# A cross network on one core: the first rows loaded by columns, and the corner matmuls behind the row tiles

## The chip, the core and the metric

The kernel runs on one core of a Trainium2 chip. The metric is the device time of one execution in microseconds. The core has a matrix engine (TensorE, PE in the profile; its weight loads are PEld), three engines for elementwise work (VectorE or DVE, ScalarE or ACT, GpSimd or POOL), a synchronisation engine (SyncE or SP) and 16 DMA engines. Loads are issued here from SP and from ScalarE, each into a queue of its own.

## The reference

Six cross layers of a recommender network, on 4096 rows of 416 features, all in bfloat16:

```python
B, F, D, L = 4096, 26, 16, 6
Din = min(F * D, 1024)          # 416
# x0: (B, Din), ws: (L, Din, Din), bs: (L, Din)
x = x0
for l in range(ws.shape[0]):
    x = x0 * (x @ ws[l] + bs[l]) + x
return x
```

The kernel uses that, up to rounding, x after layer l is x0 times a factor that grows by x @ ws + bs in each layer. It keeps x @ ws accumulated over the layers in PSUM, with the biases summed up over the layers.

## The kernel before

**Layout.** Activations lie transposed: features on the 128 partitions, rows along the free dimension. The 416 features are three chunks of 128 (0, 1, 2) and a rest of 32, called the tail. The 4096 rows are four groups (p) of 1024, each of two blocks of 512. The tail of a group's four quarters of 256 rows lies packed on 4×32 partitions. A layer's weights therefore fall into four kinds of matmul:

- *mains*: chunk by chunk, 128×128 pieces of the weights, written as 32-column tiles four at a time (`main`, with `columns` at L330 and `again` at L310, which uses the weights already held). Layer 0 of the first group, first block, is done instead in `first` with whole 128×128 matmuls (L288).
- *row tiles*: from the tail to the three chunks, 32-row tiles (L391).
- *column tiles*: from the three chunks to the tail, 32-column tiles (L406).
- the *corner*: from the tail to the tail, as a block-diagonal 128×128 matrix `wc_sb` in 32-column tiles (L387, recorded at the helper's L330). ScalarE builds it out of `w3_sb`, four copies a layer (`corner`, L531).

**Order.** For each group p and layer l, with n = 6p + l: mains of block 0, then `tail` (corner, row tiles, column tiles), then mains of block 1. The order is written out by hand and kept by semaphores. TensorE counts up `s_pe` four times a layer: behind the row tiles, behind the column tiles, and behind the second and third chunk of block 1. VectorE waits for these and forms the next x in six steps a layer (L490, L499). ScalarE (L545) and GpSimd (L234) share a seventh piece, the third chunk of block 0.

**The start.** The first 512 rows come in row-major form (`xin_sb`) in two loads of 256 rows, one from SP (L135), one from ScalarE (L516). TensorE issues 22 warm-up matmuls on ones (`idle`, L244), then transposes the rows chunk by chunk (`turn`, L256, four transposes each), and VectorE copies each transposed chunk from PSUM to `x0T_sb` (L473). `biases` (L265, L271) sums up the biases of the layers with seven small matmuls; VectorE copies these to `cb_sb` (L478). `first` then runs layer 0's mains chunk by chunk (k = 0, 1, 2), each behind its weights (`s_w0[k]`) and its copied chunk (`s_ev`). Turn 2 and two transposes of the tails (L299) stand behind the mains of k = 0. The rest of the first 1024 rows is transposed by a DMA (L144), and SP's queue then has the weights of the layers 1 to 5 (L148 for the chunks, L151 for the tail weights). Layer 0's tail weights come in four loads of 26 KB (`tails0`, L77), two from SP and two from ScalarE.

## Time and profile before

| what | value |
|---|---|
| runs | 131.56, 132.18, 132.2 us; median 132.18 |
| the profiled execution | 131.24 us, its span 129.5 us |
| mean granted clock of TensorE | 0.994 |
| TensorE busy | 124.4 us (96%) |
| VectorE busy | 93.7 us (72%) |
| ScalarE, GpSimd busy | 25.5 us (20%), 30.2 us (23%) |
| TensorE on the chain of waits | 93% |

The span goes from the first to the last instruction; the execution's time has some 1.7 us around it. The three runs are without a profile. Times in the text are microseconds from the start of the span. Matmuls overlap in the array, so the length of one (0.27 us for 256 columns) is longer than the distance between the starts of two (0.11 us at full clock). Line numbers are those of the kernel before.

### The profile page before, as it was taken

What the parts mean: (1) busy time and instruction counts of PE and PEld (TensorE: products, weight loads), DVE (VectorE), ACT (ScalarE), POOL (GpSimd) and SP (SyncE); (2) the same over time, 40 slices, a digit from 0 to 9 for tenths busy, and PEclk for the clock granted to TensorE, in tenths of its full rate; (3) what the DMA queues carried; (4) which work ended last, traced back from release to release, by engine and by line L of the source; (5) the groups of instructions that cost most, each with busy time, mean ns of one, the idle gap of its engine ahead of it and who ended that gap; (6) DMA issues with size and microseconds to landing.
All of it is one profiled execution on the core that took longest, in us unless ns stands there. A gap on an engine that the chain in (4) does not pass through costs nothing.

```text
span 129.5 us, 6917 instructions
## 1 busy us (share of the span) xinstructions
PE 124.4 (96%) x4089; PEld 66.0 (51%) x2433; DVE 93.7 (72%) x151; ACT 25.5 (20%) x55; POOL 30.2 (23%) x35
## 2 busy tenths in 40 slices
PE   6999999999999999999999999999999999999980
PEld 6754554554554554554554554554554554545660
DVE  0357967868868768769769669669669669669680
ACT  1442430431220220220220210210201201202270
POOL 5111312312302303303303303303303303203200
PEclk9999999999999999999999999999999999999997
DMA  3898787867988900997000957000000958000027
GB/s 121 220 231 244 187 124 85 127 81 108 111 77 120 113 15 15 179 69 250 23 10 15 125 123 255 21 5 0 5 20 5 135 118 267 1 5 5 0 75 189
DMA packets 35483, 12.56 MB, mean 97 GB/s; under 512 B 27770, under 2 KB 35456, under 8 KB 35456
## 3 DMA queue, kind: packets, MB, share of 16 engines
q1 hardware_dynamic: 34560, 11.84, 49.9%
q8 instruction: 25, 0.41, 1.4%
q10 hardware_dynamic: 896, 0.30, 0.9%
q14 instruction: 2, 0.02, 0.0%
HBM read 3.22 MB, written 3.41 MB: 51 GB/s over the span
## 4 chain that ended last, share of the span: by engine, by line
PE 93%; DMA 2%; DVE 2%; issue 0%
PE ps L330 37%; PE ps L310 35%; PE ps L406 8%; PE ps L391 8%; DMA xin_sb<-in_x_dram 2%; DVE xo_sb L490 2%; PE ps L288 2%; PE ps L320 1%; PE ps L256 1%; PE ps L419 0%; DVE o_sb L512 0%; PE ps L265 0%; PE ps L271 0%; PE ps L299 0%
## 5 line engine op out<-in xcount | busy, mean ns | idle before, releaser
L490 DVE SCALAR_TENSOR_TENSOR xT_sb<-ps,cb_sb,x0T_sb 128x512 bf16<-128x512 f32 x100 | 69.9, 745 | 22.7 <-PE ps L391 22.7
L330 PE MATMUL ps<-xT_sb,w_sb 128*32 128x256 bf16 x1404 | 78.1, 273 | 0.0
L310 PE MATMUL ps<-xT_sb,w_sb 128*32 128x256 bf16 x1404 | 78.1, 273 | 0.0
L330 PEld LDWEIGHTS ps<-xT_sb,w_sb 128*32 128x32 bf16 x1404 | 37.6, 97 | 37.0
L234 POOL TENSOR_TENSOR xT_sb<-t_sb,x0T_sb 128x512 bf16<-128x512 f32 x20 | 23.1, 1157 | 75.8 <-ACT t_sb L545 75.8
L545 ACT ACTIVATE t_sb<-ps,cb_sb 128x512 f32<-128x512 f32 x24 | 16.5, 687 | 91.9 <-PE ps L391 91.9
L490 DVE SCALAR_TENSOR_TENSOR xo_sb<-ps,cb_sb,x0T_sb 128x512 bf16<-128x512 f32 x20 | 14.1, 746 | 4.7 <-PE ps L391 4.5
L310 PE MATMUL ps<-x0T_sb,w_sb 128*32 128x256 bf16 x252 | 14.2, 273 | 0.0
L330 PE MATMUL ps<-x0T_sb,w_sb 128*32 128x256 bf16 x252 | 14.2, 273 | 0.0
L406 PE MATMUL ps<-xT_sb,w_sb 128*32 128x256 bf16 x240 | 10.2, 276 | 0.0
L391 PE MATMUL ps<-xt_sb,w_sb 32*128 32x256 bf16 x240 | 10.1, 271 | 0.0
L330 PEld LDWEIGHTS ps<-x0T_sb,w_sb 128*32 128x32 bf16 x252 | 6.7, 97 | 6.6
L499 DVE SCALAR_TENSOR_TENSOR xt_sb<-ps,cb_sb,x0t_sb 128x256 bf16<-128x256 f32 x20 | 9.5, 475 | 0.0
L234 POOL TENSOR_TENSOR xo_sb<-t_sb,x0T_sb 128x512 bf16<-128x512 f32 x4 | 4.6, 1154 | 15.1 <-ACT t_sb L545 15.1
L406 PEld LDWEIGHTS ps<-xT_sb,w_sb 128*32 128x32 bf16 x240 | 4.5, 95 | 4.3 <-issue 4.2
L391 PEld LDWEIGHTS ps<-xt_sb,w_sb 32*128 32x128 bf16 x240 | 4.4, 92 | 4.4 <-issue 4.2
L531 ACT ACTIVATE wc_sb<-w_sb 32x32 bf16<-32x32 bf16 x24 | 5.4, 223 | 4.4 <-DMA w_sb<-in_ws_dram 4.0
L330 PE MATMUL ps<-xt_sb,wc_sb 128*32 128x256 bf16 x80 | 5.7, 273 | 0.0
L473 DVE COPY x0T_sb<-ps 128x512 bf16<-128x512 bf16 x3 | 1.3, 424 | 5.3 <-PE ps L256 5.3
L244 PE MATMUL ps<-ones_sb 128*128 128x128 bf16 x22 | 2.5, 313 | 1.1 <-POOL ones_sb L210 1.1
L330 PEld LDWEIGHTS ps<-xt_sb,wc_sb 128*32 128x32 bf16 x80 | 2.1, 97 | 2.2
L244 PEld LDWEIGHTS ps<-ones_sb 128*128 128x128 bf16 x22 | 2.3, 148 | 1.1 <-POOL ones_sb L210 1.1
(41 smaller groups left out, 33.3 us busy)
## 6 DMA issues: line engine op xcount, KB each, us to landing
out_dram<-o_sb SPq DMA_DIRECT2D x3, 832.0 KB, 5.7
w_sb<-in_ws_dram SPq DMA_DIRECT2D x5, 312.0 KB, 6.3
w_sb<-in_ws_dram SPq DMA_DIRECT2D x8, 104.0 KB, 2.9
out_dram<-o_sb SPq DMA_DIRECT2D x2, 256.0 KB, 2.4
out_dram<-o_sb SPq DMA_DIRECT2D x2, 160.0 KB, 2.4
xin_sb<-in_x_dram ACTq DMA_DIRECT2D x1, 208.0 KB, 3.2
xin_sb<-in_x_dram SPq DMA_DIRECT2D x1, 208.0 KB, 2.9
x0T_sb<-in_x_dram SPq DMA_TRANSPOSE x13, 4.3
```

What stands on the lines that cost most here:

```text
L234: pool.tensor_tensor(out=xdst(p, l, 0, 2), in0=t_sb[:, n % 2, :], in1=x0c(p, 0, 2), op=ALU.mult,).then_inc(s_pl, 1)
L244: pe.matmul(ps[:, 0, 0:128], lhsT=ones_sb[:, :], rhs=ones_sb[:, :], start=True, stop=True,)
L288: pe.matmul(chunk(h, m), lhsT=w_sb[:, 0, k, m * 128:(m + 1) * 128], rhs=xsrc(0, 0, 0, k)[:, h * NT:(h + 1) * NT], start=(k == 0 and m != 1 ...
L310: return pe.add_instruction(mybir.InstMatmult(name="I-%d" % (1000000 + count[0]), engine=mybir.EngineType.PE, start_tensor_calc=start, sto ...
L330: ins = pe.matmul(out[c:c + 32, :], lhsT=lhsT[:, c:c + 32], rhs=rhs, start=start, stop=stop, skip_group_check=True, tile_position=(0, c),)
L391: ins = pe.matmul(chunk(g, m), lhsT=w3_sb[32 * g:32 * g + 32, l, m * 128:(m + 1) * 128], rhs=xt[32 * g:32 * g + 32, :], start=(l == 0 and ...
L406: ins = pe.matmul(ps_tail[32 * g:32 * g + 32, :], lhsT=w_sb[:, l, k, DF:D], rhs=xsrc(p, l, g // 2, k)[:, (g % 2) * NT:(g % 2 + 1) * NT], s ...
L473: dve.tensor_copy(out=x0T_sb[:, c, 0:NB], in_=psT[:, 4 + c, 0:NB]).then_inc(s_ev, 1)
L490: dve.scalar_tensor_tensor(out=halves(xdst(p, l, blk, c)), in0=chunk2(blk, c), scalar=cb_sb[:, c, l:l + 1], in1=halves(x0c(p, blk, c)), op ...
L499: dve.scalar_tensor_tensor(out=tdst(p, l), in0=ps_tail, scalar=cb_sb[:, 3, l:l + 1], in1=x0t_sb[:, p, :], op0=ALU.add, op1=ALU.mult,).then ...
L531: act.activation(out=wc_sb[32 * g:32 * g + 32, l, 32 * g:32 * g + 32], in_=w3_sb[32 * g:32 * g + 32, l, DF:D], func=ACTF.Copy,).then_inc(s ...
L545: act.activation(out=halves(t_sb[:, n % 2, :]), in_=chunk2(0, 2), func=ACTF.Identity, bias=cb_sb[:, 2, l:l + 1],).then_inc(s_act, 1)
```

## The change

Four things change, at the start of the kernel and in `tail`:

- The first 512 rows are split by columns: SP loads columns 0 to 127 of all 512 rows (all that turn 0 needs), ScalarE columns 128 to 415. Turn 0 waits for the first load, turn 1 for the second.
- The order in `first` is turn 0, biases, turn 1, mains, where it was turn 0, turn 1, biases, mains. VectorE's copy of the biases moves ahead of its copy of chunk 1.
- The warm-up has 18 matmuls and not 22. Of the four loads of layer 0's tail weights, SP issues one and ScalarE three.
- In `tail`, the corner stands behind the row tiles, ahead of the column tiles. The row tiles wait for the tail weights themselves (`s_wt`), and the corner alone for ScalarE's copies (`s_wc`). The row tile (3, 2) of layer 0 now starts the accumulation in the PSUM bank that it shares with `ps_tail`.

```diff
+        def rows(e, i):
+            c0, c1 = ((0, 128), (128, D))[i]
+            e.dma_start(
+                xin_sb[:, :, c0:c1], x0[0:NB, c0:c1].rearrange("(j b) d -> b j d", b=128)
+            ).then_inc(s_xin[i], 16)
...
-            sp.dma_start(
-                xin_sb[:, 0:2, :], x0[0:256, :].rearrange("(j b) d -> b j d", b=128)
-            ).then_inc(s_xin[0], 16)
+            rows(sp, 0)
...
-            tails0(sp, 0)
+            tails0(sp, (0,))
...
-            idle(22)
+            idle(18)
             pe.wait_ge(s_setup, 3)
             def turn(c):
+                if c < 2:
+                    pe.wait_ge(s_xin[c], 16)
                 for j in range(4):
-                    if c == 0 and j % 2 == 0:
-                        pe.wait_ge(s_xin[j // 2], 16)
...
                 turn(0)
+                biases()
                 turn(1)
-                biases()
                 for k in range(3):
...
                 if n == 0:
                     pe.wait_ge(s_ev, 4)
-                    pe.wait_ge(s_cb, 1)
-                    pe.wait_ge(s_wc, 4)
+                    pe.wait_ge(s_wt[0], 64)
                 elif l == 0:
                     pe.wait_ge(s_x0t[p], 16)
                 elif n < L:
-                    pe.wait_ge(s_wc, 4 * n + 4)
+                    pe.wait_ge(s_wt[n], 16)
...
-                columns(ps_tail, wc_sb[:, l, :], xt, start=(l == 0), stop=False)
...
-                            start=(l == 0 and (g, m) in ((2, 0), (2, 2), (3, 0))),
+                            start=(l == 0 and (g, m) in ((2, 0), (2, 2), (3, 0), (3, 2))),
...
                 ins.then_inc(s_pe, 1)
+
+                if n < L:
+                    pe.wait_ge(s_wc, 4 * n + 4)
+                columns(ps_tail, wc_sb[:, l, :], xt, start=False, stop=False)
...
             for c in range(3):
-                dve.wait_ge(s_inT, (1, 2, 4)[c])
+                dve.wait_ge(s_inT, (1, 3, 4)[c])
...
-                if c == 1:
-                    dve.wait_ge(s_inT, 3)
+                if c == 0:
+                    dve.wait_ge(s_inT, 2)
...
-            act.dma_start(
-                xin_sb[:, 2:4, :], x0[256:512, :].rearrange("(j b) d -> b j d", b=128)
-            ).then_inc(s_xin[1], 16)
+            rows(act, 1)
...
-            tails0(act, 2)
+            tails0(act, (1, 2, 3))
```

More of the change, by code (lines that the diff above doesn't have):

```diff
@@ L72, in chunk2, with tails0 @@
             return ps_q[:, blk, m // 2, :, m % 2, :]
-        def tails0(e, g0):
-            for g in (g0, g0 + 1):
+        def rows(e, i):
[3 more added lines that the diff above has]
+            ).then_inc(s_xin[i], 16)
+        def tails0(e, groups):
+            for g in groups:
                 e.dma_start(w3_sb[32 * g:32 * g + 32, 0, :], ws[0, DF:D, :]).then_inc(s_wt[0], 16)
```

## The prediction

> **What bounds the kernel now.** I read the page first: TensorE is busy in all slices but the first and the last, and nearly the whole chain of waits is its matmuls.

> ```profile
> PE   6999999999999999999999999999999999999980
> PE 93%; DMA 2%; DVE 2%; issue 0%
> ```

> So two things move the end: when the dense matmuls begin, and how many slots of TensorE a layer takes. Next the chain of waits in order of time, over the first 8.6 us (start, length, what):

> ```profile
> 0.80 2.88 DMA xin_sb<-in_x_dram
> 3.69 0.14 issue
> 3.82 1.09 PE ps L256 x8
> 4.91 0.17 PE ps L265 x3
> 5.08 0.11 PE ps L271 x4
> 5.19 0.76 PE ps L288 x6
> 5.95 0.22 PE ps L256 x4
> ```

> The first load lands at 3.69; then come two turns (eight transposes), the seven bias matmuls and the first mains (L288, the first of them at 5.12 in the timeline). The pace shows too: eight transposes take 1.09 us, four later ones 0.22. By the starts of single matmuls, 128 columns take 107 ns until about 5.0 and 55 ns after. The granted clock is recorded as full from 5.03, 3.97 us behind the first warm-up matmul (1.06), and not recorded before. Mains that start earlier run at half pace.

> Third, the timeline of a tail in the steady state:

> ```profile
> 12.46 0.28 PE L330 MATMUL ps<-xt_sb,wc_sb 128*32 128x256 bf16 x4
> 12.68 0.51 PE L391 MATMUL ps<-xt_sb,w_sb 32*128 32x256 bf16 x12
> 13.11 0.51 PE L406 MATMUL ps<-xT_sb,w_sb 128*32 128x256 bf16 x12
> 13.45 0.28 PE L330 MATMUL ps<-xT_sb,w_sb 128*32 128x256 bf16 x4
> ```

> Four tiles side by side take one slot of 0.11. The corner is one slot, the row tiles and the column tiles three each, yet the corner lasts 0.22 and the row tiles 0.43: every change of tile shape leaves 0.10 empty. A layer is 43 slots and two such changes, 4.92 us.

> Fourth, the loads (KB, us from issue to landing):

> ```profile
> xin_sb<-in_x_dram ACTq DMA_DIRECT2D x1, 208.0 KB, 3.2
> xin_sb<-in_x_dram SPq DMA_DIRECT2D x1, 208.0 KB, 2.9
> w_sb<-in_ws_dram SPq DMA_DIRECT2D x1, 312.0 KB, 4.4
> x0T_sb<-in_x_dram SPq DMA_TRANSPOSE x1, 3.7
> ```

> The second half of the rows lands at 4.05 (0.80+3.2). The last two rows are layer 1's weights (issued at 5.66, landed at 10.02) and the transposed second block (issued at 4.05, landed at 7.75).

> **The two loads by columns.** The first becomes 128 KB in 512 pieces of 256 bytes, the second 288 KB in 512 pieces of 576; before, each was 256 pieces of 832. In the trace's packets a piece of 832 bytes took 39 ns and one of 256 (the transposes) 18, so by a straight line one of 576 takes about 30. For each of the 16 DMA engines that is 16×39 = 0.62 us a load before, and 32×18 = 0.58 and 32×30 = 0.96 after. On one engine the time from a load's first packet to its last was about 1.5 times the packets' own (0.95 for 0.62). So the first load gains 1.5×0.04 = 0.06 and the second loses 1.5×0.34 = 0.5. Bounds for the first load: by bytes alone 3.69 − 0.96×(1 − 128/208) = 3.32; by the number of pieces alone 3.69+0.96 = 4.65. For the second: 4.05 if only the sum of bytes counts, 5.0 by pieces. I take 3.55 and 4.45, near what the packets say, leaning to bytes since the two loads share the engines and together ran at 377 GB/s at their best. The row says that a 256-byte piece moves 14 bytes a ns against 21 for 832, a mild loss. [...]

> **TensorE's order at the start.** Now turn 0, biases, turn 1, mains; the new order of instructions has turn 1 still ahead of the first mains, so the biases and half the transposes are what moves under the second load. Turn 0: 3.55+0.13 (landing to transpose, as at 3.69 and 3.82) = 3.68, four at 0.107, to 4.11. The biases wait for their own load, which stands behind the first rows on SP's queue: it landed at 4.08, 0.4 behind the rows, and I take 3.95 to 4.1, so it is just not late. They start at 4.24 (0.14 of change of shape, as between 4.70 and 4.84) and last 0.28 (4.84 to 5.12): 4.52. Turn 1 waits for 4.45 + 0.08 = 4.53, and ends at 4.96. The mains then start at 4.96 instead of 5.12; layer 0's first weights landed at 4.59, the copy of chunk 0 needs 0.42 from about 4.2. Gain 0.16. With the second load at its bounds: at 4.05 the biases are the limit, turn 1 ends at about 4.95 and the gain is no larger; at 5.0 the mains start at about 5.4, a loss of 0.25.

> **Queues moved past.** On VectorE the copy of the biases (0.17) comes ahead of the copy of chunk 1; that copy is wanted one stage of mains and a turn (1.0 us) later, which hides it. GpSimd's two copies of row tails wait for both loads and now end near 5.2; they are wanted at about 5.85. SP issues one tail load less (0.47), so its transposes and layer 1's weights go out up to 0.47 earlier; TensorE would want them 0.26 earlier, at 7.93 and 10.13, against landings of 7.75 and 10.02 before, so they are still in time even if they don't move. ScalarE issues one more (0.5), ahead of its table load and the corner copies; those ended at 7.22 and are wanted at about 7.5, behind the row tiles. Row tiles now wait for the tail weights directly (11.18 for layer 1, wanted at 12.4).

> **Four warm-up matmuls less.** 4×0.107 = 0.43 that end at 2.99 instead of 3.42, in time that waits for the load: nothing on the path, but less activity ahead of the clock (a rival below).

> **The corner behind the row tiles.** In the first tail whole-array mains come before it: before, three changes of shape (0.09, 0.12 and 0.10 by the starts 7.33, 7.53, 7.76, 8.19), after, two: −0.10, once. In the 23 other tails the row tiles now follow column-shaped mains and the corner joins the column tiles: two changes as before, 0. The measured changes differ by ±0.02, so 23 tails bound this at ±0.46. VectorE and ScalarE get the row tiles' signal one slot (0.11) earlier; VectorE already ends 0.2 ahead of the next tail (12.18 against 12.36), so nothing follows. At the end of the kernel VectorE's last steps wait for the mains of L320, so nothing follows there either.

> **Sum:** −0.16 − 0.10 = −0.26 on the profiled execution's 131.24 (span 129.5), 130.98. The runs' median is 132.18, 0.94 above that execution; with the same difference, 131.9. A difference of 0.5% (0.66 us) is about what can be told from no change, so this is within it.

> **Rivals.**

> *The clock opens later* (slower). TensorE stood idle for 0.64 us (3.38 to 3.79, and two short gaps) before 5.03; after, it idles 0.69 from 2.99 to 3.68 alone, and more at each load. If the count of warm time starts over at the turns, the clock opens 3.97 behind 3.68, at 7.65, and the mains from 4.96 run at half pace: (7.65 − 5.03)/2 − 0.26 = +1.05, 133.2. It decides once the gap is too long; in the trace 0.41 did not do it. If only busy time counts, the opening moves by about 0.2 and costs 0.1. [...] Chance 0.24.

> *The second load is late*, at 5.0: mains at 5.4, +0.25 − 0.10 = +0.15, 132.3. For it speaks that both loads double their pieces. Chance 0.14; a fifth of that goes past +0.66, should the later loads on the same engines slip as well.

> *Layer 1's weights had been late in the timed runs* (faster). They landed 0.37 before use in an execution that is 0.94 faster than the median; one DMA engine's share landed 1.0 behind the other fifteen. If they bind in the runs, SP's 0.47 comes on top: −0.73, 131.45. Against it: the profile shows no such wait. Chance 0.15.

> *The change doesn't do what its words say:* the first mains don't pass turn 1. That is in the order and in my sum already.

> **How the numbers follow.** The forecast gets 0.47. Faster by over 0.5%: 0.15, the weights' rival. Slower: 0.25, of it 0.22 from the clock (its smaller forms stay within 0.5%) and 0.03 from the late load. Within: 0.60. The forecast's own range is 131.4 to 132.4 (the ±0.46 of the tails). The whole range goes from 131.3 (the weights' rival) to 133.0, which leaves out the full restart of the clock and little more.

> **What would show it.** Right: first load landing at 3.4 to 3.7, second at 4.3 to 4.6, first main at 4.9 to 5.05, the clock recorded from about 5.0; in the first tail L391's successor starts straight behind the mains with a single gap of 0.2, and layers keep 4.92. Wrong: 128 columns still at 107 ns behind 5.5; a wait of TensorE for the second load until 4.8 or later; a layer cadence other than 4.92; a wait for layer 1's weights at about 10.

## The result, and the profile after

The changed kernel took 133.18 us (median of 6 executions, 133.01 to 133.7), the kernel before 132.06 (6 executions, 131.56 to 132.46): a ratio of 1.0094, 95% interval 1.0065 to 1.0123. It is slower, by 1.1 us. The profiled execution took 133.18 us with a span of 131.2, against 131.24 and 129.5 before. The ratios leave out executions that are over 1.5% above the fastest of the same kernel, which in the kernel before are up to 18 of 28 and part of what is at work here, so the means below are over all executions of a kernel.

The engine on the chain is the same as before:

```profile
PE 92%; DMA 2%; DVE 2%; SPq 0%; issue 0%
```

The chain of waits in order of time, over the first 10 us of the changed kernel:

```profile
1.32 3.04 DMA bsa_sb<-in_bs_dram
4.37 0.05 issue
4.41 0.24 PE ps L270 x3
4.65 0.12 PE ps L276 x3
4.77 0.54 PE ps L261 x4
5.31 1.28 PE ps L293 x6
6.59 0.43 PE ps L261 x4
7.02 0.21 PE ps L304 x2
7.23 2.05 PE ps L293 x12
9.28 0.44 PE ps L393 x12
```

Two pieces of the same chain before, behind those that the prediction shows:

```profile
6.29 1.31 PE ps L288 x12
7.83 0.44 PE ps L391 x12
```

Two things are to be seen. The chain no longer starts with a load of rows but with the biases' load, which landed at 4.37; turn 1 stands behind the biases. And the pace: the six mains take 1.28 us where six took 0.76 before, the turn behind them 0.43 instead of 0.22, the last twelve mains 2.05 instead of 1.31. TensorE runs at half pace until far into the last mains: 0.213 us from one main to the next, where it was 0.109. The trace records the full clock from 8.63; it was 5.03 before. In the timeline the first row tile starts at 9.21, 1.46 later than before.

The loads landed as follows (KB, us from issue; the third line is layer 1's weights, issued at 5.43):

```profile
xin_sb<-in_x_dram ACTq DMA_DIRECT2D x1, 288.0 KB, 3.4
xin_sb<-in_x_dram SPq DMA_DIRECT2D x1, 128.0 KB, 2.8
w_sb<-in_ws_dram SPq DMA_DIRECT2D x1, 312.0 KB, 3.6
```

And the timeline of a tail in the steady state:

```profile
14.13 0.51 PE L393 MATMUL ps<-xt_sb,w_sb 32*128 32x256 bf16 x12
14.57 0.29 PE L335 MATMUL ps<-xt_sb,wc_sb 128*32 128x256 bf16 x4
14.69 0.50 PE L412 MATMUL ps<-xT_sb,w_sb 128*32 128x256 bf16 x12
15.02 0.28 PE L335 MATMUL ps<-xT_sb,w_sb 128*32 128x256 bf16 x4
```

The corner now runs straight on into the column tiles (0.12), and the empty slot of 0.10 stands once ahead of the row tiles and once behind them. From row tile to row tile a layer takes 4.92 us, as before, in 22 of 23 cases (one is 5.02). So the span's +1.68 is made of 1.46 at the first row tile, 0.11 because the corner now follows that row tile, and 0.10 in that one layer.

### The profile page after: what moved, and what is told of

Its sections match the earlier page's. It is cut to its first block, busy times and chain, and to the rows that moved or that the text cites. A ratio compares the mean times of both kernels' runs of the same rounds, so it can differ in the third digit from the quotient of the medians.

```text
span 131.2 us, 6909 instructions
## 1 busy us (share of the span) xinstructions
PE 125.7 (96%) x4085; PEld 67.1 (51%) x2429; DVE 95.2 (73%) x151; ACT 25.4 (19%) x55; POOL 30.4 (23%) x35
## 3 DMA queue, kind: packets, MB, share of 16 engines
HBM read 3.22 MB, written 3.41 MB: 50 GB/s over the span
## 4 chain that ended last, share of the span: by engine, by line
PE 92%; DMA 2%; DVE 2%; SPq 0%; issue 0%
PE ps L335 39%; PE ps L315 34%; PE ps L393 8%; PE ps L412 6%; PE ps L293 3%; DMA bsa_sb<-in_bs_dram 2%; DVE xo_sb L496 2%; PE ps L325 1%; PE ps L261 1%; PE ps L425 0%; SPq L77 0%; DVE o_sb L518 0%; PE ps L270 0%; PE ps L304 0%; PE ps L276 0%
## 5 line engine op out<-in xcount | busy, mean ns | idle before, releaser
L496 DVE SCALAR_TENSOR_TENSOR xT_sb<-ps,cb_sb,x0T_sb 128x512 bf16<-128x512 f32 x100 | 71.2, 745 | 22.2 <-PE ps L393 21.4
L335 PEld LDWEIGHTS ps<-xT_sb,w_sb 128*32 128x32 bf16 x1404 | 38.0, 97 | 36.7
L412 PEld LDWEIGHTS ps<-xT_sb,w_sb 128*32 128x32 bf16 x240 | 6.4, 97 | 0.1
L293 PE MATMUL ps<-x0T_sb,w_sb 128*128 128x256 bf16 x18 | 3.7, 383 | 0.0
## 6 DMA issues: line engine op xcount, KB each, us to landing
w_sb<-in_ws_dram SPq DMA_DIRECT2D x5, 312.0 KB, 5.6
```

Source lines behind the costliest of these rows:

```text
L293: pe.matmul(chunk(h, m), lhsT=w_sb[:, 0, k, m * 128:(m + 1) * 128], rhs=xsrc(0, 0, 0, k)[:, h * NT:(h + 1) * NT], start=(k == 0 and m != 1 ...
L335: ins = pe.matmul(out[c:c + 32, :], lhsT=lhsT[:, c:c + 32], rhs=rhs, start=start, stop=stop, skip_group_check=True, tile_position=(0, c),)
L412: ins = pe.matmul(ps_tail[32 * g:32 * g + 32, :], lhsT=w_sb[:, l, k, DF:D], rhs=xsrc(p, l, g // 2, k)[:, (g % 2) * NT:(g % 2 + 1) * NT], s ...
L496: dve.scalar_tensor_tensor(out=halves(xdst(p, l, blk, c)), in0=chunk2(blk, c), scalar=cb_sb[:, c, l:l + 1], in1=halves(x0c(p, blk, c)), op ...
```

## The experiments

Theory A is the clock: TensorE's idle time at the start decides when the full clock comes. Theory B is the loads by columns, which make other loads land later. Theory C is the corner's place.

### Each part alone

Four kernels ran on one chip: `idle(18)` set back to `idle(22)` in the changed kernel (first), and in the kernel before `idle(22)` set to `idle(18)` (second), the corner moved alone (third), and the rows loaded by columns alone (fourth).

```diff
-            idle(18)
+            idle(22)
```

> The changed kernel with 22 warm-up matmuls again instead of 18, nothing else. Theory A (the clock: four warm-ups less make TensorE too idle in the span that decides, so the full clock comes 3.6 us later, at 8.63 and not at 5.03, and the first mains run at half pace): the clock opens near 5.0 again, the first row tile stands near 7.6 and the time is 131.7 to 132.0, that is 1.1 to 1.4 below the changed kernel and 0.1 to 0.3 below the kernel before. Theory B (the loads by columns make biases, tails and late weights land later, and the clock is only a companion): the time stays at 133.0 to 133.3. Theory C (the corner behind the row tiles costs something in every tail): stays above 132.7.

> The kernel before with 18 warm-up matmuls instead of 22, nothing else. Theory A in its plain form (the count of warm-ups decides alone): the clock opens near 8.6 and the time rises to 133.0 to 133.4. Theory A in its weaker form (warm-ups and the later gap at the biases together decide): opens near 5.0, time 132.0. Theories B and C: no change, 131.9 to 132.2, the clock at 5.0.

> The kernel before with the corner matmuls behind the row tiles in every tail, nothing else. Theory A and B: 0.1 faster in the first tail (two changes of tile shape and not three) and no more, so 131.9 to 132.2. Theory C: some hundredths in each of 24 tails, so 132.6 to 133.2 with a layer cadence above 4.92.

> The kernel before with the first rows loaded by columns (128 and 288 columns), nothing else: turn 0, turn 1, biases as before, 22 warm-ups, two tail loads from each queue. Theory A: the clock opens near 5.0; the second load lands at about 4.16 and turn 1 waits little, so 132.0 to 132.3. Theory B: later landings of biases (4.37) and layer 0's third weights (6.4) set the mains back by 0.3 or more at full clock, so 132.4 to 133.0.

| kernel | clock opens in its profile | mean of all (from, to) | ratio to before (95%) |
|---|---|---|---|
| changed, 22 warm-ups | 9.78 | 132.96 (131.94, 134.49) | 1.0 (0.9956, 1.0044) |
| before, 18 warm-ups | 7.24 | 133.29 (132.5, 134.34) | 1.0031 (0.9986, 1.0077) |
| before, corner moved | 7.30 | 132.36 (131.41, 133.88) | 0.9958 (0.9912, 1.0005) |
| before, rows by columns | 9.79 | 133.03 (131.94, 134.1) | 1.0003 (0.9957, 1.0049) |
| before | | 133.21 (131.8, 134.23), 35 executions | |

Most expectations missed, and for one reason: the kernel before is itself no fixed base. Its 35 executions spread over 2.4 us, and the clock's opening in these four profiles lies between 7.2 and 9.8, earliest in the one with 18 warm-ups. Four warm-ups are not the whole story: taken from the kernel before they cost 0.08 (95% by resampling the executions: −0.31 to 0.50), and given back to the changed kernel they did not bring its clock to 5.0. Nor do the loads by columns alone cost anything that shows (−0.18, −0.67 to 0.30). What fell is theory C: with the corner moved, most layers still take 4.92 and the time does not rise. It falls, by 0.85 (0.33 to 1.36), more than the 0.1 that I expected; why so much is not shown, but one likely part is found further down.

### What opens the clock

The recorded stretches of full clock last 122.88 us (the kernel before and the changed kernel among them), 126.29 or 133.12: 36, 37 and 39 times 3.413. I read that as a clock that was decided once every 3.41 us in these runs. I then took, for each of the sixteen profiles on normal starts, the share of time in which TensorE streams columns (107 ns for 128), in the 3.41 us that end at the opening and in the 3.41 us before those:

| profile | opens | last 3.41 us busy | the 3.41 us before |
|---|---|---|---|
| before | 5.03 | 77% | 16% |
| changed | 8.63 | 100% | 63% |
| changed, 22 warm-ups | 9.78 | 97% | 73% |
| before, 18 warm-ups | 7.24 | 84% | 55% |
| before, corner moved | 7.30 | 87% | 68% |
| before, rows by columns | 9.79 | 97% | 72% |
| the ten others, below | 3.82 to 9.16 | 78% to 100% | 0% to 66% |

All sixteen fit one reading: the clock opened at the first end of a 3.41 us stretch whose busy share lay above a line between 73% (the highest that did not open it) and 77% (the lowest that did), and where the stretches began differed from profile to profile (openings from 3.82 to 9.79). The line is fitted to these sixteen profiles, and with matmuls that start close together laid end to end it comes to 79% and 75% instead. The 81% of the expectations below is an estimate from a rougher count. The opening goes along with the time: the five of these profiles whose clock opened by 5.15 took 131.24 to 132.05 us, the four that opened behind 8.6 took 133.18 to 134.1. In the kernel before, the gap ahead of turn 0 (3.38 to 3.82) and the small ones behind it leave a stretch just above or just below that line (77% in the profile that opened at 5.03); so, as I read the spread of its times, it opens early in some executions and one stretch later in others. In the changed kernel TensorE idles from 2.96 to 3.72 and again from 4.10 to 4.41, and by that reading no stretch that holds both can pass (at least 1.07 of 3.41 idle, so at most 69% busy). The next runs test that.

### The gap filled

The changed kernel again, with long warm-ups ahead of everything (below), and with the idle time filled:

```diff
-            idle(18)
+            idle(25)
...
                 turn(0)
+                idle(3)
                 biases()
```

> The changed kernel as it is, beside the kernel before on one chip, in more executions. Four profiles so far opened the clock at 7.2 to 9.8 and two kernels share all values, so theory A is now: the clock opens at the first end of a free-running span of 3.41 us in which TensorE was busy for about 81% or more; its phase is random, and the idle time at the start decides whether the first such span or the next one qualifies. The changed kernel idles 1.1 us between 2.96 and 4.66, so only spans that begin behind these gaps qualify: openings from 6.8 to 10.2, mean 8.5, and times from 131.9 to 134.0. The kernel before (0.65 us of idle time) is at the edge: openings from 4.4 to 10.2. So changed minus before is between 0 and +1.2 on this chip, by where its loads land. Theory B: +0.9 or more, with a spread no larger than that of the kernel before.

> The changed kernel with the idle time at the start filled: 25 warm-ups ahead of turn 0 instead of 18, and 3 between turn 0 and the biases. Theory A: any span of 3.41 us from the first warm-up on is then over 81% busy, so the clock opens between 3.9 and 7.3, mean 5.6; the mean cost over an opening at 5.1 falls from about 1.7 to 0.3 us, so 1.2 to 1.5 below the changed kernel and 0.5 to 1.3 below the kernel before on the same chip, with all executions in a band of 1.2 us. Theory B: no gain (the warm-ups stand in waiting time only), or 0.1 slower.

On one chip the changed kernel took 133.67 in the mean (132.74 to 134.53, 6 executions; ratio to before 1.0136, 1.0078 to 1.0194), the kernel before 132.86 (131.32 to 134.13, 17), and the changed kernel with the filled start 132.21 (131.66 to 132.91, 12). Seven warm-ups ahead of turn 0 and three behind it, nearly all in time that waited for loads, took 1.46 us off (0.91 to 1.98), and all twelve lie within 1.25 us. The clock opened at 5.15 in the profile. That is what theory A expected and theory B excluded. The changed kernel has no execution below 132.7, and the kernel before has eight of seventeen; two of the six lie above the 134.0 that I gave as the end of the changed kernel's range.

The other direction, on the kernel before: 26 warm-ups, and 12.

```diff
-            idle(22)
+            idle(26)
```

> The kernel before with 26 warm-ups instead of 22, nothing else: they end at 3.85, when the rows land, so the 0.44 us of idle time ahead of turn 0 is gone. Theory A: any span of 3.41 us is then over 88% busy, the clock opens between 3.9 and 7.3 in every execution, the late ones (9 to 10) disappear: no execution above 132.9, mean 131.8 to 132.1, 0.7 to 1.0 below the mean of the kernel before. If the clock were not the lever: 0 to 0.1 slower.

> The kernel before with 12 warm-ups instead of 22, nothing else: TensorE idles from 2.35 to 3.9. Theory A: no span that holds this gap qualifies, as in the changed kernel; openings from 6.9 to 10.3, no execution below 132.2, mean 133.4 to 133.8, as for the changed kernel (133.67), with nothing of the loads or the tail changed. If the loads or the tail make the changed kernel slow: mean as before, 132.9.

The chain of waits with 26 warm-ups:

```profile
1.06 2.95 PE ps L244 x26
4.02 1.04 PE ps L256 x8
5.05 0.17 PE ps L265 x3
5.22 0.12 PE ps L271 x2
5.34 1.18 PE ps L288 x6
6.53 0.22 PE ps L256 x4
6.75 0.11 PE ps L299 x2
6.86 1.31 PE ps L288 x12
```

and with 12:

```profile
5.37 1.39 PE ps L288 x6
6.76 0.43 PE ps L256 x4
7.19 0.21 PE ps L299 x2
7.40 2.23 PE ps L288 x12
```

The mains start at the same time; the turn between them takes 0.22 in one and 0.43 in the other. With 26 the clock opens at 6.18, with 12 at 9.16. The means on that chip are 132.43 (132.0 to 133.44) with 26, 133.21 (132.43 to 133.88) with 12, and 133.35 for the kernel before (28 executions): 26 warm-ups bring 0.92 (0.55 to 1.27). That is as expected in size, but the mean with 26 is above the 131.8 to 132.1 that I wrote, as is the mean of the kernel before on this chip, and one execution lies above 132.9, at 133.44, where I expected none. The ratio for 26 warm-ups is 0.9992 (0.9946 to 1.0038): the whole gain is that the times above 133.44, 18 of 28 in the kernel before, no longer occur. With 12 no execution is below 132.4, as expected, but the mean is below the 133.4 to 133.8 that I wrote, and no worse than the kernel before (−0.15, −0.54 to 0.27), whose times suggest that its gap failed in most executions on this chip. So this run agrees with theory A without proving it; the filled starts carry it.

### The path with the clock open

To take the clock out, both kernels got 130 warm-ups ahead of the first load and 48 more while the rows come:

```diff
+            sp.wait_ge(s_go, 1)
...
+            act.wait_ge(s_go, 1)
...
-            idle(22)
+            idle(130).then_inc(s_go, 1)
+            idle(48)
```

> The kernel before, with 130 warm-up matmuls ahead of everything: SP and ScalarE wait for them before their first load, and 48 more warm-ups bridge the time until the rows land. The clock is then open before any of the work, in every execution. The time is longer by the 8 to 11 us of warm-ups; only the difference to the next run counts, and the spread should shrink to that of the warm-ups' own end.

> The changed kernel with the same 130 and 48 warm-ups. All that differs from the run before is then the path at full clock, measured from the first load's issue. Theory A: -0.1 (the first tail's change of shape, and nothing from the loads, because the biases' load, which landed 3.57 behind the first issue, now bounds the turn: 3.57+0.05+0.3+0.22 = 4.1 against 3.25+0.04+0.33+0.45 = 4.1 before). The prediction's own sum: -0.26. Theory B: +0.3 or more. Theory C: +0.4 or more, with a layer cadence above 4.92.

The times, 142.26 and 142.72 in the mean, hold the warm-up's own random length; their difference, 0.46 (−0.25 to 1.11), decides nothing. In the profiles, counted from the first load's issue, the first main comes 0.12 earlier with the change (4.22 against 4.35) and the end 0.52 earlier (129.09 against 129.61), of which 0.20 are two odd layers of the other kernel. Each kernel's chain shows what the first corner then waits for. Before:

```profile
14.02 3.22 DMA w_sb<-in_ws_dram
18.45 0.29 PE ps L333 x4
```

Changed:

```profile
13.31 4.15 DMA w_sb<-in_ws_dram
18.58 0.29 PE ps L338 x4
```

The load is the last of layer 0's tail weights to land; ScalarE's four copies stand between it and the corner. (All four loads count up one semaphore; the profile puts the last landing down to SP's, but can't tell it from ScalarE's.) It landed 6.50 behind the first issue in the changed kernel and 6.00 in the kernel before. The filled kernel shows the same wait without long warm-ups (idle time and its releaser in brackets):

```profile
8.43 0.29 PE L336 MATMUL ps<-x0t_sb,wc_sb 128*32 128x256 bf16 x4 [0.22 <-ACT wc_sb L536]
```

This makes the tail loads a second suspect. Two more kernels: the corner's move with 26 warm-ups and the kernel before's loads, and the filled kernel with the tail loads two and two.

```diff
-            tails0(sp, (0,))
+            tails0(sp, (0, 1))
...
-            tails0(act, (1, 2, 3))
+            tails0(act, (2, 3))
```

> The kernel before with the corner behind the row tiles and 26 warm-ups: the rows, the tail loads and the order at the start stay as they were. A candidate that may beat both kernels. Theory A: 0.1 to 0.3 below the run with 26 warm-ups alone (one change of shape less, and row tiles that don't wait for ScalarE's copies when the clock opens early), so a mean of 131.6 to 131.9. If the corner's move costs in every tail: 0.4 or more above that run.

> The changed kernel with the filled start (25 and 3 warm-ups) and with layer 0's tail loads shared two and two again, as in the kernel before. In the runs so far these loads all landed 5.4 to 6.0 us behind the first issue with two and two, and 6.1 to 6.8 with three from ScalarE, and with an open clock the first corner waited 0.3 to 0.6 for them. Theory: the corner's wait shrinks by 0.2 to 0.5 in executions with an early clock, so the mean falls to 131.8 to 132.1 (132.21 with three). If the tail loads don't bind: 132.2.

Both beat the kernel before on their chip (133.35): 131.97 (6 executions; ratio 0.9891, 0.9846 to 0.9936) and 132.22 (11; 0.9925, 0.9887 to 0.9962). The second missed its expected mean, and its base had run on another chip. So all four kernels with filled starts ran once more, on one chip:

> The changed kernel with the filled start (25 and 3 warm-ups), once more, beside the next three on one chip. Theory A with the path gain that the pair behind long warm-ups showed (-0.3 to -0.5): mean 0.2 to 0.4 below the kernel before with 26 warm-ups. If the later landing of the other loads (layer 0's third weights 0.9 later, tail loads 0.7 later) eats the gain: equal to it within 0.1.

> The kernel before with 26 warm-ups, as the base for the other three: mean 132.2 to 132.5, no execution above 133.5.

> The kernel before with 26 warm-ups and the corner behind the row tiles: 0.1 to 0.4 below the run with 26 warm-ups alone (131.97 against 132.43 on another chip, six and twelve executions). If it is only the one change of tile shape: 0.1.

> The changed kernel with the filled start and layer 0's tail loads two and two: 0.1 to 0.4 below the same with three from ScalarE, if the first corner's wait of about 0.4 (profiled at 8.43 against 7.94) sets the end whenever the clock opens before about 6.5; equal if the layers behind it wait for something else by then.

| kernel, filled start, 12 executions each | mean (from, to) | ratio to before (95%) |
|---|---|---|
| changed loads and corner | 132.59 (132.0, 133.04) | 1.0008 (0.9972, 1.0044) |
| before | 132.31 (131.76, 132.68) | 1.0 (0.9963, 1.0037) |
| before, corner moved | 132.06 (131.46, 132.43) | 0.9951 (0.9916, 0.9986) |
| changed, tail loads two and two | 132.09 (131.45, 133.32) | 0.9943 (0.9901, 0.9985) |
| kernel before as it is, 35 executions | 132.94 (131.49, 134.15) | |

With filled starts the whole change is 0.28 slower (0.04 to 0.52), not faster; the gain that I expected does not show. But this is not the change alone, for the three dummy matmuls behind turn 0 hold up the biases. In the profile of the first kernel of the table the biases' load landed at 4.44, and TensorE came to them 0.30 later:

```profile
4.28 0.52 PE L249 MATMUL ps<-ones_sb 128*128 128x128 bf16 x3
4.74 0.23 PE L270 MATMUL ps<-u_sb,bsa_sb 7*128 7x6 bf16 x3
```

In the changed kernel without them it came 0.05 behind the landing. So up to 0.25 of the 0.28 can be the filling's own, and what the change does to the path at an equal clock stays open. The corner's move brings 0.24 (0.00 to 0.48); on the chip before it was 0.47 (0.17 to 0.79), so it is probably worth more than the 0.10 of one change of shape. One reason is in the profile of the kernel before with 26 warm-ups, whose clock opened at 3.82: its first corner waited for ScalarE's copies, and with the corner moved the row tiles run in that time.

```profile
7.88 0.29 PE L330 MATMUL ps<-x0t_sb,wc_sb 128*32 128x256 bf16 x4 [0.20 <-ACT wc_sb L531]
```

Three tail loads on ScalarE's queue instead of two cost 0.50 (0.10 to 0.86) here; the same pair on two chips had shown nothing (132.21 and 132.22). With two and two the changed kernel equals the corner's move alone (+0.03, −0.34 to +0.41), so the loads by columns and the new order bring nothing that shows, with the dummies' delay in it (in that profile TensorE came to the biases 0.31 behind their landing). Where the 0.50 lies is only half shown: in the first pair of profiles (clock at 3.94 and 5.15) the first corner starts 7.14 behind the first issue with two and two and 7.63 with three, as the wait would have it; in the second pair (5.91 and 6.02) it starts at 7.76 in both.

One thing stays open: in about two thirds of the profiles single layers, mostly between the third and the eighth, take 0.1 to 0.7 longer, at places without a releaser in the profile. They add to the spread, by 1.46 in the worst profile (133.32 us, with the clock at 5.91), and are not explained here.

## Why the prediction was wrong

I predicted 131.9 in a range of 131.3 to 133.0, with 0.60 on no difference; it is 133.18. The step that failed is "four warm-up matmuls less": nothing on the path, I wrote, only less activity ahead of the clock. The sum put that activity at 0, and it was the larger term: the clock opened at 8.63 instead of 5.03, which makes up nearly all of the span's +1.68 (worked out below). What failed was less the four matmuls than the idle time that they were part of, 0.76 us ahead of turn 0 and 0.31 ahead of the biases: ten dummy matmuls in it took 1.46 off, while four alone, taken from the kernel before, cost 0.08 with an interval around nothing. How much of the 1.1 us the four make is not shown.

- **The clock.** The rival was named, with 133.2 as its time, but it got 0.24, and the range was drawn so as to leave it out. Two readings were behind that. I took the opening at 5.03 as a property of the kernel, while it was one draw: it came early in that execution, with 77% busy where 73% has failed elsewhere. And I looked for a gap that resets the count, while the sixteen profiles fit a share of a 3.41 us stretch; by that reading 0.41 of idle time was nearly too much. The price by it is (8.63 − 5.10)/2 = 1.76 less the 0.10 of the tail, against 1.58 in the span without the odd layer. (The prediction's 2.99 and 3.42 for the end of the warm-ups are 2.96 and 3.38 in the traces; nothing hangs on it.) The median of 132.18 against 131.24 in the profile was a hint that openings vary, and I used it for another rival (layer 1's weights), which no profile supports: in the changed kernel they landed at 8.99, wanted at 12.0.
- **The loads.** The first landed at 3.59 (I took 3.55), the second at 4.16 (4.45, with 4.05 as the bound by bytes). The number of pieces counted less than I gave it; a piece of 256 bytes took 18 ns, as the transposes' did, and one of 576 took 29. The biases' load was the mis-sized term: it landed at 4.37 and not at 3.95 to 4.1, and this goes with the loads by columns: on one chip it landed at 4.57 with them alone, and at 4.16 and 4.25 with the rows as before, and the profiles on the other chips agree. So turn 1 waited for the biases and not for the rows, and the first main started at 5.10 instead of 4.96: a gain of 0.02 for 0.16.
- **Queues moved past.** I wrote that ScalarE's corner copies would end in time; they ended at 7.98 instead of about 7.2. In the profiled execution the late clock hid that. With filled starts on one chip the third load on ScalarE cost 0.50, more than the rest of the change earned there. Of the loads behind the rows I priced SP's earlier issue alone; what the loads do to each other I left out: their packets took 1.10 times the 16 DMA engines' time from 3.0 to 5.1 and 1.04 times from 5.1 to 8.62 (1.01 and 0.86 before), and layer 0's last weights landed at 6.44 instead of 5.51.
- **The tail.** Right: no cost in the layers (4.92 before and after), one change of shape less in the first tail. With filled starts the move was worth 0.24 and 0.47; the first interval holds the 0.10, the second does not. The sum lacked the first corner's wait for ScalarE's copies when the clock opens early.
- **What would show it wrong** was the right list: 128 columns were still at 107 ns behind 5.5.

## What to carry to other kernels

Before a short prologue on TensorE is moved, count how busy it is ahead of the recorded opening of the clock (here in stretches of 3.41 us: 77% opened it, 73% did not), and fill the waits with dummy matmuls up to the moment the data lands and no further: ten dummy matmuls, nearly all in waiting time, were worth 1.46 us here, more than every reordering tried, though the three ahead of the biases ran on past the landing, by up to 0.27. One profile shows one draw of the clock's opening (3.82 to 9.79 over the sixteen here); where executions of the same kernel spread by 2 us, get several profiles and compare means on one chip before a 0.3 us step is believed. When a load is handed to another queue, follow who waits for it once everything ahead of it is faster.
